# Seven-product stage one of a mixture of experts: product 4 ahead of product 3, product 2 summed onto product 4's PSUM bank

## The chip, the cores and the metric

The kernel runs on one core of a Trainium2 chip. The metric is the device time of one execution in microseconds (us). Before the change the median of three runs is 2261.65 us (2260.79 to 2263.05).

The engines are TensorE (PE; its weight loads are shown apart as PEld), VectorE (DVE), ScalarE (ACT), GpSimd (POOL) and SyncE (SP), which only issues transfers here. PSUM is the memory that the matmuls write; the kernel uses it as eight banks of 128 x 512 fp32.

## The reference

Attention with a block mask on 4 x 8 heads of 768 tokens gives x, 3072 tokens of 512 features. A mixture of 8 experts follows, with every token sent to every expert, and with gate weights P that are balanced by rows and columns in eight rounds:

```python
for e in range(E):
    h = np.maximum(x @ w1[e], 0.0)
    ye = h @ w2[e]
    out += P[:, e:e + 1] * ye
```

w1[e] is 512 x 1024, w2[e] is 1024 x 512.

## The kernel before

The attention fills the first 422 us of the profile. The rest, to 2257 us, is the mixture of experts, of which the change touches the first product, x @ w1.

**The arithmetic.** Both products are taken as 2 x 2 blocks by a scheme of seven products in place of eight (numbered 0 to 6), with sums and differences of blocks ahead and behind. Every operand is kept as an fp16 high half and an fp16 low half, and a product is the sum of three passes, high by high, high by low and low by high.

**Items, quarters, products.** The work is cut into 32 items i, which are expert e = i // 4 and batch b = i % 4. `stage1(i, qi)` makes a quarter of an item, 128 of the 512 columns of a block. Its seven products, in the order 0, 1, 5, 6, 3, 4, 2, are six matmuls of 128 x 384 each (L1200) into a bank of the pool `ps_h`, which has four banks and in which a tile is a product (`p4_0_1` is product 4 of quarter 1 of item 0). `comb` (L1212) is VectorE's `scalar_tensor_tensor`: PSUM times 2^-20 plus a tile in SBUF. With P0 to P6 the products:

- a1 = P0 (ScalarE, L1247); r11 = P1 + a1; a1 = a1 + P5; u3 = P6 + a1
- c21 = P3 + u3; then two combs read product 4's bank: u3 = P4 + u3 and a1 = P4 + a1
- a1 = P2 + a1
- relu of r11, u3, a1 (L1251, L1267, L1271); `add` makes the four sums that stage two needs on GpSimd (L1274, L1086).

These tiles come from a pool of eight (`fresh`). `emit(n, src)` turns one of them into an operand of stage two, a tile h out of 30: the high half on ScalarE (L1222), the low half on VectorE (L1226, L1232) or, for 2, 3 and 5, on GpSimd.

`stage2(i, p)` (L1302) takes product p of the second stage in three tiles `py`, twelve matmuls of 128 x 256 each (L1317), into the pool `ps_y`, the other four banks; VectorE adds them to the output (L1340, tiles `acc`).

**The order of the work.** The main loop runs stage two of item i, its products 0, 1, 5, 6, 3, 4, 2, with the four quarters of item i + 1 between them. Lazy work is placed by `Slots`, a planner in Python: `tick(n, m)` charges a product 0.976 us of TensorE, 0.55 n of VectorE and 0.5 m of ScalarE, and queued work is handed out when the engines' charges leave room. That work is: the low halves; the balance of the gate (L1144 to 1180); and, once an expert, the *exchange* of weights. In an exchange w1 or w2 of the next expert is loaded (L177, 2 MB), its largest magnitude is taken in eight pieces on ScalarE (L108, tile `mx_w`), reduced on VectorE (L194, `ma_w`), spread over the partitions by TensorE (L114, `all_w`), and made a scale (L200 to 206). Then each of the seven sums of weight blocks is split into halves, the high one on ScalarE (L1064) and the low one on VectorE (L1068), as `w1p` (in `arena` and `attic`) and `w2p`. At an exchange of w1 the split of product p is queued by `used[p]()`, behind the matmuls of product p that use the old weights. While these sit in the queues, the inputs of the last batch are split too (L355 on ScalarE, L356 on VectorE, tiles `xs_3`), at the start of stage one. Each item's x is loaded by SyncE in the order 0, 1, 5, 6, 3, 4, 2 (L227).

Behind the planner a scheduler reorders the instructions of each engine by its own costs; the order shown below is what comes out of both. An engine runs its instructions in that order, one after the other, each when the semaphores of its operands allow.

## Time and profile before

| | |
|---|---|
| median of three runs | 2261.65 us |
| span of the profiled execution, its own time from first to last instruction | 2260.3 us |
| stage one of the experts begins | 422 us |
| TensorE busy | 2168.3 us (96%) |
| VectorE busy | 1873.6 us (83%) |
| ScalarE, GpSimd busy | 1314.1 us, 1326.1 us |
| mean granted TensorE clock | 0.995 |

The profile is of one execution. A row of a group gives line, engine, operation, out<-in, its shape and count, then busy time, the mean time of one in nanoseconds, and the idle time of the engine ahead of them with what ended it. Rows of the timeline give start, duration and operation, and in brackets the idle time ahead and its releaser. Names are the program's without numbers: `p<-attic` is a product of stage one, `a<-p,a` a comb. Matmuls overlap, so the duration of a single one is longer than the spacing of a row of them. "PEclk" and the clock of a window are the share of TensorE's full clock that was granted.

### The profile page before, as it was taken

To read this page: it belongs to the slowest core of one execution; us is meant where nothing else is said; L and a number is where in the kernel's file an instruction comes from. 1 tells how busy PE (TensorE), PEld (TensorE's weight loads), DVE (VectorE), ACT (ScalarE), POOL (GpSimd) and SP (SyncE) were. 2 spreads that over 40 slices of the span, in tenths; PEclk is the share of its full clock that TensorE was granted. 3 is DMA by queue.
4 is the path that set the end of the run, shared out by engine and by line. 5 is a ranking of instruction groups with operands and counts; after the bars stand their busy time and mean duration, and the time that the engine had idled before them with its cause. 6 is when DMAs were issued, how large, how long until landed. Compare 5 with 4: busy or idle time off the path is not lost.

```text
span 2260.3 us, 47619 instructions
## 1 busy us (share of the span) xinstructions
PE 2168.3 (96%) x18892; PEld 1599.6 (71%) x18892; DVE 1873.6 (83%) x3289; ACT 1314.1 (58%) x2431; POOL 1326.1 (59%) x1369
## 2 busy tenths in 40 slices
PE   6999999899988999999999999999999999999999
PEld 4777667567775777677777777777777777777777
DVE  7889999787888878887888788878887888788876
ACT  6888889664457544654465446544654465446442
POOL 3124456585549564866486548655866586658553
PEclk9999999999999999999999999999999999999999
DMA  7766965313122212121212121212121212121221
GB/s 165 143 151 144 203 134 134 115 57 115 50 63 74 87 50 69 68 88 50 86 51 87 50 87 50 87 50 87 50 87 50 87 50 87 50 87 57 78 78 50
DMA packets 195347, 192.36 MB, mean 85 GB/s; under 512 B 132124, under 2 KB 150580, under 8 KB 195124
## 3 DMA queue, kind: packets, MB, share of 16 engines
q1 hardware_dynamic: 194560, 189.30, 29.0%
q8 instruction: 147, 2.41, 0.4%
q14 instruction: 76, 0.62, 0.1%
q10 hardware_dynamic: 564, 0.03, 0.0%
HBM read 140.54 MB, written 17.30 MB: 70 GB/s over the span
## 4 chain that ended last, share of the span: by engine, by line
PE 71%; DVE 11%; POOL 10%; ACT 4%; issue 3%; DMA 1%; SPq 0%; POOLq 0%; DVEq 0%; ACTq 0%
PE p L1200 30%; PE py L1317 30%; POOL r L1079 3%; PE u L760 3%; DVE acc L1340 2%; PE t L705 2%; PE m L669 2%; PE m L672 2%; PE t L702 2%; POOL h L1232 2%; DVE top L678 1%; DVE attic L1068 1%; DVE h L1232 1%; POOL s L1274 1%; POOL a L1086 1%
## 5 line engine op out<-in xcount | busy, mean ns | idle before, releaser
L1317 PE MATMUL py<-w2p,h 128*128 128x256 f16 x8064 | 945.0, 273 | 31.2 <-DVE acc L1340 14.7
L1317 PEld LDWEIGHTS <-h 128*128 128x128 f16 x8064 | 787.7, 98 | 165.7 <-issue 32.2
L1340 DVE SCALAR_TENSOR_TENSOR acc<-py,spare,acc 128x256 f32<-128x256 f32 (+1 forms) x840 | 456.1, 580 | 64.5 <-PE py L1317 60.0
L1232 POOL TENSOR_TENSOR h<-u,h 128x384 f16<-128x384 f32 x128 | 119.8, 936 | 578.4 <-ACT h L1222 578.3
L1200 PEld LDWEIGHTS <-attic 128*128 128x128 f16 x3072 | 300.6, 98 | 198.2 <-issue 19.9
L1200 PE MATMUL p<-attic 128*128 128x384 f16 x2304 | 411.5, 326 | 11.2 <-DVE a L1212 5.3
L1200 PE MATMUL p<-arena 128*128 128x384 f16 x2304 | 413.3, 328 | 5.1 <-DVE arena L1068 4.2
L1200 PEld LDWEIGHTS <-arena 128*128 128x128 f16 x2304 | 226.4, 99 | 140.9 <-issue 7.4
L1222 ACT ACTIVATE h<-c 128x384 f16<-128x384 f32 x256 | 133.0, 520 | 316.2 <-DVE c L1212 240.7
L1212 DVE SCALAR_TENSOR_TENSOR a<-p,a 128x384 f32<-128x384 f32 x384 | 210.8, 549 | 21.3 <-PE p L1200 17.1
L678 DVE TENSOR_REDUCE top<-m 128x1 f32<-128x768 f32 x192 | 181.7, 950 | 31.4 <-PE m L672 30.9
L710 ACT ACTIVATE pe<-t,qk 128x768 int32<-128x768 f32 x192 | 172.1, 899 | 45.3 <-PE t L705 42.3
L1222 ACT ACTIVATE h<-r 128x384 f16<-128x384 f32 x256 | 132.3, 519 | 66.4 <-POOL r L1086 61.9
L1086 POOL TENSOR_TENSOR c<-c,r 128x384 f32<-128x384 f32 x128 | 159.9, 1249 | 10.0
L1086 POOL TENSOR_TENSOR r<-s,r 128x384 f32<-128x384 f32 x128 | 153.8, 1201 | 10.0
L1212 DVE SCALAR_TENSOR_TENSOR r<-p,a 128x384 f32<-128x384 f32 x128 | 70.7, 552 | 95.1 <-PE p L1200 71.2
L1200 PE MATMUL p<-arena,attic 128*128 128x384 f16 x768 | 146.0, 326 | 3.3 <-DVE a L1212 3.3
L1274 POOL TENSOR_TENSOR s<-a,u 128x384 f32<-128x384 f32 x128 | 134.4, 1050 | 21.8 <-ACT a L1271 21.8
L1222 ACT ACTIVATE h<-s 128x384 f16<-128x384 f32 x128 | 66.7, 521 | 134.6 <-POOL s L1274 134.5
L1086 POOL TENSOR_TENSOR a<-a,r 128x384 f32<-128x384 f32 x128 | 135.5, 1059 | 9.5
L1079 POOL TENSOR_TENSOR r<-r 128x256 f32<-128x256 f32 (+1 forms) x106 | 119.7, 1148 | 34.4 <-DVE arena L1068 33.2
L1232 POOL TENSOR_TENSOR h<-r,h 128x384 f16<-128x384 f32 x128 | 136.9, 1070 | 3.8 <-ACT h L1222 2.8
(205 smaller groups left out, 3723.5 us busy)
## 6 DMA issues: line engine op xcount, KB each, us to landing
arena<-xd SPq DMA_DIRECT2D x128, 384.0 KB, 4.0
attic<-xd SPq DMA_DIRECT2D x96, 384.0 KB, 4.3
r<-in_moe_w_dram SPq DMA_DIRECT2D x16, 2048.0 KB, 8.9
arena<-in_q_dram SPq DMA_DIRECT2D x16, 384.0 KB, 4.2
arena<-in_k_dram SPq DMA_DIRECT2D x16, 384.0 KB, 4.4
arena<-in_v_dram SPq DMA_DIRECT2D x4, 1536.0 KB, 8.2
xd<-xs_t SPq DMA_DIRECT2D x16, 384.0 KB, 3.5
out_dram<-acc SPq DMA_DIRECT2D x48, 128.0 KB, 1.7
```

The costliest lines, as they stand in the source:

```text
L678: nc.vector.tensor_reduce(out=tops[n][:, c : c + 1], in_=sc[:, :S], axis=AX.X, op=ALU.max)
L710: nc.scalar.activation(pe, sc[:, :S], AF.Exp, bias=EXP_SHIFT, scale=qk[n // 2][3])
L760: nc.tensor.matmul(uv[:, c], lhsT=l[:, c * P : (c + 1) * P], rhs=w[:, h, kc, :], start=(kc == 0 and c == 0 and m == 0), stop=(kc == NC - 1 ...
L1079: lambda c=c: Pinned.gpsimd.tensor_tensor(out=out[:, c], in0=x[:, c], in1=y[:, c], op=op),
L1086: nc.gpsimd.tensor_tensor(out=out, in0=x, in1=y, op=ALU.subtract)
L1200: nc.tensor.matmul(ps, lhsT=w1p[p][:, l, kc, fs], rhs=xp[p][:, r, kc], start=(kc == 0 and m == 0), stop=(kc == KH - 1 and m == 2),)
L1212: nc.vector.scalar_tensor_tensor(out=t, in0=ps, scalar=HDOWN, in1=other, op0=ALU.mult, op1=ALU.add)
L1222: nc.scalar.activation(h[:, 0], src, AF.Relu if relu else AF.Copy)
L1232: eng.tensor_tensor(out=h[:, 1], in0=src, in1=h[:, 0], op=ALU.subtract)
L1274: nc.gpsimd.tensor_tensor(out=s1, in0=a1, in1=u3, op=ALU.add)
L1317: nc.tensor.matmul(py, lhsT=hs[i, p, kc][:, l, tsl], rhs=w2p[p][:, r, kc], start=(kc == 0 and m == 0), stop=(kc == KF // 2 - 1 and m == 2),)
L1340: nc.vector.scalar_tensor_tensor(out=dst, in0=src, scalar=c, in1=dst, op0=ALU.mult, op1=ALU.add)
```

## The change

Product 4 is taken ahead of product 3. It is combined into a new tile c22 = P4 + u3, whose relu and high half follow at once; c21 = P3 + u3 is then written over u3. Product 2 opens no bank of its own: its matmuls add to what stands in product 4's bank (`start=False`), once the comb of c22 has read it, and one comb a1 = (P4 + P2) + a1 takes the place of two. A quarter has one comb less, 128 in all, and takes six banks and not seven; the number of matmuls and of tiles stays. The planner is charged for it: `tick(2, 2)` and `tick(1, 1)` become `tick(1, 2)` and `tick(1, 1)`, 0.55 less of VectorE a quarter.

```diff
@@ -1192,14 +1192,17 @@
         fs = slice(qi * P, (qi + 1) * P)
         lop = LOPE if i < NLE else LOP
 
-        def product(p):
+        def product(p, ps=None):
             slots.need(("w1", i // B, p))
-            ps = ps_h.tile([P, 512], F32, tag="ph", name=f"p{p}_{i}_{qi}")[:, :TH]
+            opens = ps is None
+            if opens:
+                ps = ps_h.tile([P, 512], F32, tag="ph", name=f"p{p}_{i}_{qi}")[:, :TH]
             for kc in range(KH):
                 for m, (l, r) in enumerate(((0, 0), (0, 1), (1, 0))):
                     nc.tensor.matmul(
                         ps, lhsT=w1p[p][:, l, kc, fs], rhs=xp[p][:, r, kc],
-                        start=(kc == 0 and m == 0), stop=(kc == KH - 1 and m == 2),
+                        start=(opens and kc == 0 and m == 0),
+                        stop=(kc == KH - 1 and m == 2), skip_group_check=True,
                     )
             if used and p in used:
                 used[p]()
@@ -1257,21 +1260,21 @@
         comb(u3, product(6), a1)
         tick(1, 0)
         slots.settle(i, qi - 1)
-        c21 = fresh("c21")
+        c22 = fresh("c22")
+        p4 = product(4)
+        comb(c22, p4, u3)
+        nc.scalar.activation(c22, c22, AF.Relu)
+        emit(3, c22)
+        tick(1, 2)
+        c21 = u3
         comb(c21, product(3), u3)
         emit(1, c21, relu=True)
         tick(1, 1)
-        p5 = product(4)
-        comb(u3, p5, u3)
-        comb(a1, p5, a1)
-        nc.scalar.activation(u3, u3, AF.Relu)
-        emit(3, u3)
-        tick(2, 2)
-        comb(a1, product(2), a1)
+        comb(a1, product(2, p4), a1)
         nc.scalar.activation(a1, a1, AF.Relu)
 
         def add():
-            nc.gpsimd.tensor_tensor(out=s1, in0=a1, in1=u3, op=ALU.add)
+            nc.gpsimd.tensor_tensor(out=s1, in0=a1, in1=c22, op=ALU.add)
             sub(a1, a1, r11)
             slots.need((("h", i, 0), i, qi))
             sub(r11, s1, r11)
```

By the edit the planner hands work out at other places, and the scheduler orders all engines anew. Three places are shown, of before and then of after. In the changed kernel lines below L1195 have numbers higher by two or three (L1212 becomes L1215, L1340 becomes L1343); product 2's matmuls and comb carry the tile of product 4.

First, ScalarE at the first exchange of w2 (expert 0 to 1, `mx_w2_1`), at the end of item 4's stage one. `h` are high halves, `acc` the scaling of the output. Before, from the high half of quarter 4_3's c21 on:

```order
L1222 ACTIVATE h_15_8087<-c21_4_3_11290 128x384
L1267 ACTIVATE u3_4_3_11279<-u3_4_3_11279 128x384
L1222 ACTIVATE h_0_8072<-c21_4_2_11118 128x384
L108 ACTIVATE unread_80,mx_w2_1_10773<-r2_1_10770 128x512
L1271 ACTIVATE a1_4_3_11251<-a1_4_3_11251 128x384
L1222 ACTIVATE h_23_8095<-u3_4_3_11279 128x384
L1279 ACTIVATE c21_4_3_11290<-c21_4_3_11290 128x384
L1323 ACTIVATE acc_0_8102<-acc_0_8102,spare_3_10729 128x512 x2
L108 ACTIVATE unread_80,mx_w2_1_10773<-r2_1_10770 128x512
```

After, from the high half of quarter 4_1's a1 on, past the last L108:

```order
L1225 ACTIVATE h_16_8088<-a1_4_1_10859 128x384
L1225 ACTIVATE h_14_8086<-r11_4_2_11053 128x384
L1225 ACTIVATE h_18_8090<-r11_4_1_10869 128x384
L108 ACTIVATE unread_80,mx_w2_1_10741<-r2_1_10738 128x512
L1225 ACTIVATE h_0_8072<-u3_4_1_10896 128x384
L1266 ACTIVATE c22_4_2_11083<-c22_4_2_11083 128x384
L108 ACTIVATE unread_80,mx_w2_1_10741<-r2_1_10738 128x512
L1225 ACTIVATE h_27_8099<-u3_4_2_11072 128x384
L1225 ACTIVATE h_8_8080<-c22_4_2_11083 128x384
L1282 ACTIVATE u3_4_2_11072<-u3_4_2_11072 128x384
L1274 ACTIVATE a1_4_2_11044<-a1_4_2_11044 128x384
L1250 ACTIVATE a1_4_3_11215<-p0_4_3_11216 128x384
```

The last L108 of `mx_w2_1` stood behind the relu of quarter 4_3's c21 and a scaling of acc; it stands behind c22 of 4_2, ahead of a1 of 4_3.

Second, VectorE at the start of stage one, around the end of quarter 1 of item 0. Before:

```order
L1212 SCALAR_TENSOR_TENSOR u3_0_1_8216<-p4_0_1_8239,u3_0_1_8216 128x384
L1212 SCALAR_TENSOR_TENSOR a1_0_1_8181<-p4_0_1_8239,a1_0_1_8181 128x384
L204 RECIPROCAL sw2_0_7715<-ma_w2_0_7714 128x1
L1226 SCALAR_TENSOR_TENSOR h_8_8080<-c21_0_1_8227,h_8_8080 128x384
L1212 SCALAR_TENSOR_TENSOR a1_0_1_8181<-p2_0_1_8251,a1_0_1_8181 128x384
L205 TENSOR_SCALAR sw2_0_7715<-sw2_0_7715 128x1
L206 TENSOR_SCALAR iw2_0_7716<-ma_w2_0_7714 128x1
L1353 TENSOR_SCALAR pc_0_10725<-iw1_0_4252,iw2_0_7716 128x1
L1355 TENSOR_SCALAR pcb_0_10727<-inv_v_72,pc_0_10725 128x4
L356 TENSOR_TENSOR xs_3_b10_9225<-xf_3_6802,xs_3_b10_9225 128x768
L356 TENSOR_TENSOR xs_3_b01_9276<-xf_3_6802,xs_3_b01_9276 128x768
L1212 SCALAR_TENSOR_TENSOR r11_0_2_8276<-p1_0_2_8277,a1_0_2_8266 128x384
```

After:

```order
L1215 SCALAR_TENSOR_TENSOR c22_0_1_8225<-p4_0_1_8226,u3_0_1_8214 128x384
L1358 TENSOR_SCALAR pcb_0_10519<-inv_v_72,pc_0_10517 128x4
L1235 TENSOR_TENSOR h_4_8076<-a1_0_0_8104,h_4_8076 128x384
L1215 SCALAR_TENSOR_TENSOR u3_0_1_8214<-p3_0_1_8237,u3_0_1_8214 128x384
L356 TENSOR_TENSOR xs_3_b10_9026<-xf_3_6802,xs_3_b10_9026 128x768
L356 TENSOR_TENSOR xs_3_b01_9077<-xf_3_6802,xs_3_b01_9077 128x768
L1215 SCALAR_TENSOR_TENSOR a1_0_1_8179<-p4_0_1_8226,a1_0_1_8179 128x384
L1229 SCALAR_TENSOR_TENSOR h_9_8081<-u3_0_1_8214,h_9_8081 128x384
L356 TENSOR_TENSOR xs_3_b11_9080<-xf_3_6802,xs_3_b11_9080 128x768
L1215 SCALAR_TENSOR_TENSOR r11_0_2_8272<-p1_0_2_8273,a1_0_2_8262 128x384
L1215 SCALAR_TENSOR_TENSOR a1_0_2_8262<-p5_0_2_8286,a1_0_2_8262 128x384
```

The two L356 stood behind the comb of product 2 and ahead of product 1's of the next quarter; they stand ahead of product 2's comb (`a1_0_1<-p4_0_1`), and a third L356 stands behind it.

Third, VectorE at a later exchange (w2 of expert 4). Before, from the reduction (L194) to the first steps of the scale:

```order
L194 TENSOR_REDUCE ma_w2_4_18868<-mx_w2_4_18867 128x1
L1212 SCALAR_TENSOR_TENSOR r11_16_3_19357<-p1_16_3_19358,a1_16_3_19348 128x384
L1212 SCALAR_TENSOR_TENSOR a1_16_3_19348<-p5_16_3_19369,a1_16_3_19348 128x384
L1232 TENSOR_TENSOR h_21_8093<-r11_16_3_19357,h_21_8093 128x384
L1212 SCALAR_TENSOR_TENSOR u3_16_3_19377<-p6_16_3_19378,a1_16_3_19348 128x384
L1212 SCALAR_TENSOR_TENSOR c21_16_3_19386<-p3_16_3_19387,u3_16_3_19377 128x384
L1212 SCALAR_TENSOR_TENSOR u3_16_3_19377<-p4_16_3_19399,u3_16_3_19377 128x384
L1212 SCALAR_TENSOR_TENSOR a1_16_3_19348<-p4_16_3_19399,a1_16_3_19348 128x384
L1226 SCALAR_TENSOR_TENSOR h_19_8091<-c21_16_3_19386,h_19_8091 128x384
L1212 SCALAR_TENSOR_TENSOR a1_16_3_19348<-p2_16_3_19411,a1_16_3_19348 128x384
L200 TENSOR_REDUCE ma_w2_4_18868<-all_w2_4_19397 128x1
L201 TENSOR_SCALAR ma_w2_4_18868<-ma_w2_4_18868 128x1
```

After:

```order
L194 TENSOR_REDUCE ma_w2_4_18739<-mx_w2_4_18738 128x1
L1215 SCALAR_TENSOR_TENSOR u3_16_2_19073<-p3_16_2_19095,u3_16_2_19073 128x384
L1343 SCALAR_TENSOR_TENSOR acc_3_9915<-py_15_4_0_19119,spare_6_16614,acc_3_9915 128x256 x2
L1229 SCALAR_TENSOR_TENSOR h_8_8080<-u3_16_2_19073,h_8_8080 128x384
L1343 SCALAR_TENSOR_TENSOR acc_3_9915<-py_15_4_1_19135,spare_6_16614,acc_3_9915 128x256 x2
L1215 SCALAR_TENSOR_TENSOR a1_16_2_19043<-p4_16_2_19083,a1_16_2_19043 128x384
L1343 SCALAR_TENSOR_TENSOR acc_3_9915<-py_15_4_2_19152,spare_6_16614,acc_3_9915 128x256 x2
L1343 SCALAR_TENSOR_TENSOR acc_3_9915<-py_15_2_0_19172,spare_6_16614,acc_3_9915 128x256
L1235 TENSOR_TENSOR h_25_8097<-s1_16_2_19113,h_25_8097 128x384
L1235 TENSOR_TENSOR h_16_8088<-a1_16_2_19043,h_16_8088 128x384
L1343 SCALAR_TENSOR_TENSOR acc_3_9915<-py_15_2_1_19188,spare_6_16614,acc_3_9915 128x256
L200 TENSOR_REDUCE ma_w2_4_18739<-all_w2_4_19170 128x1
```

The reduction stood ahead of quarter 16_3's combs, and the scale behind them; the reduction stands in quarter 16_2, and the scale ahead of 16_3's combs.

## The prediction

> **What bounds the kernel now.** The page comes first: how long, and which engine is never free.
>
> ```profile
> span 2260.3 us, 47619 instructions
> PE 2168.3 (96%) x18892; PEld 1599.6 (71%) x18892; DVE 1873.6 (83%) x3289; ACT 1314.1 (58%) x2431; POOL 1326.1 (59%) x1369
> L1212 DVE SCALAR_TENSOR_TENSOR a<-p,a 128x384 f32<-128x384 f32 x384 | 210.8, 549 | 21.3 <-PE p L1200 17.1
> ```
>
> TensorE is busy 96% of the span. The change takes no matmul away, so it can gain only where TensorE waits, or where its clock falls. The VectorE operation that it takes away is one of the third row's kind: 0.549 us, 128 times, 70.3 us in all, nearly all of it beside matmuls. The second view is TensorE's waits over the mixture of experts, 420 to 2260 us (columns: total, times, longest).
>
> ```profile
> PE py L1317 <- DVE acc L1340: 14.7, 11, 1.7
> PE p L1200 <- DVE a L1212: 9.5, 8, 2.7
> PE py L1317 <- DVE w2p L1068: 8.1, 7, 1.7
> PE all_w L114 <- DVE ma_w L194: 7.3, 1, 7.3
> PE py L1317 <- ACT w2p L1064: 6.6, 8, 1.0
> PE p L1200 <- DVE arena L1068: 4.2, 6, 1.9
> PE p L1200 <- ACT a L1247: 2.8, 3, 1.3
> PE p L1200 <- DVE r L1212: 2.3, 6, 1.1
> ```
>
> These sum to 55.5 us in 50 waits: that, and what the clock loses, is the ceiling of any gain. The third view is busy time by stretch (columns: stretch, length, PE, PEld, DVE, ACT, POOL, granted clock, DMA share, GB/s).
>
> ```profile
> 442.00:452.00 10.00, 5.37 (x27) 2.88 (x27) 9.31 (x14) 6.68 (x14) 9.84 (x8) 0.86 0.11 41
> 452.00:462.00 10.00, 10.00 (x51) 5.45 (x50) 8.46 (x16) 6.66 (x15) 8.22 (x9) 0.80 0.69 221
> 700.00:706.00 6.00, 0.00 (x0) 0.00 (x0) 3.65 (x6) 5.54 (x15) 5.02 (x6) 0.65 0.37 125
> 706.00:712.00 6.00, 5.60 (x18) 2.80 (x19) 5.42 (x13) 6.00 (x12) 5.84 (x8) 0.50 0.00 0
> 980.00:1100.00 120.00, 120.00 (x927) 90.46 (x925) 90.74 (x170) 57.37 (x121) 69.44 (x66) 1.00 0.20 68
> 1202.00:2100.00 898.00, 879.34 (x6707) 655.10 (x6705) 744.38 (x1304) 468.93 (x950) 578.16 (x544) 1.00 0.20 69
> ```
>
> Between exchanges of weights (980 to 1100) TensorE is busy all the time, and nothing is to be had there. What is lost lies at the start of stage one, at the first exchange of experts, and in a few microseconds at each later exchange. So the change is costed at those places, and VectorE's 70.3 us by themselves at nothing: matmuls cover them, and they cost only where VectorE is late for TensorE.
>
> **The change, part by part.**
>
> *A, the start (433 to 470 us).* TensorE's waits there, and, in the timeline (start, length, operation), VectorE's work ahead of the two longest:
>
> ```profile
> PE p L1200 <- DVE a L1212: 3.2, 3, 2.2
> PE p L1200 <- ACT a L1247: 1.6, 2, 1.3
> PE p L1200 <- DVE r L1212: 1.1, 1, 1.1
> ```
>
> ```profile
> 443.68 2.81 DVE L356 TENSOR_TENSOR xs_b<-xf,xs_b 128x768 f16<-128x768 f32 x2 [0.62 <-ACT xs_b L355]
> 446.41 0.54 DVE L1212 SCALAR_TENSOR_TENSOR r<-p,a 128x384 f32<-128x384 f32 x1
> ...
> 447.68 2.16 DVE L1232 TENSOR_TENSOR h<-a,h 128x384 f16<-128x384 f32 x1
> 449.76 0.54 DVE L1212 SCALAR_TENSOR_TENSOR a<-p,a 128x384 f32<-128x384 f32 x1
> ```
>
> 5.9 us of waiting: two L356 of the input's last batch (2.81 us) stand ahead of the comb that empties product 1's bank, and then a low half of 2.16 us ahead of the next. In the new order (second piece of the order above) the two stand between product 3's comb and product 2's. By TensorE's new order products 0, 1 and 2 of about 1 us each run meanwhile, so they cover 2.9 us. The comb of product 1 still comes late: after product 3's matmuls end, VectorE does one comb (0.56 with some 0.14 before it), 2.81, a comb of 0.54, a low half of about 1, a third L356 of about 1.4 (half of 2.81) and the comb (0.54), 7.0 us. The matmuls that need its bank, product 3 of that quarter, stand six products behind, 5.8 us. That leaves 1.2 us, so I take 4.7 us off. If the low half is again 2.16 us the gain is 3.5; if all waits go, 5.9.
>
> The clock: in the rows 442 to 462 it stood at 0.86 and 0.80, which loses 1.4 + 2.0 = 3.4 us less what falls into idle time, some 3.0. With one wait of a microsecond left I take half off, 1.5 (bounds 0 and 3.0). [...]
>
> *B, the first exchange (698.8 to 712 us).* TensorE stands 7.3 us (the fourth of the waits above) for the scale of the second expert's w2:
>
> ```profile
> 705.45 0.61 ACT L108 ACTIVATE unread<-r 128x512 bf16<-128x512 f32 x1
> 706.19 0.16 DVE L194 TENSOR_REDUCE ma_w<-mx_w 128x1 f32<-128x8 f32 x1 [2.53 <-ACT unread L108]
> ```
>
> The last of ScalarE's eight L108 ends it. The planner charges VectorE 0.55 less a quarter, so lazy work is handed out sooner; the first piece of the order above shows that the last L108 now stands behind c22 of quarter 4_2, and not behind c21 of 4_3: almost a quarter earlier, seven products of 0.98 us (three take 1307.08 to 1310.01 in part D), 6.8 us. Besides, TensorE now has product work mixed with the last matmuls of stage two of item 3, where before it ran quarters 4_0 to 4_3 bare. The 7.3 us go (bound: 0, if the load of w2, which starts behind the last split of w1, comes no earlier and ends last). With them goes the clock at 0.50 in the row 706 to 712, 5.60 busy, half lost: 2.8 us. [...] B is 10.1 us.
>
> *C, the six later exchanges.* One stretch that holds five of them, 1098 to 2100, and around one of them a split of w2 on VectorE and two of TensorE's waits:
>
> ```profile
> PE py L1317 <- DVE acc L1340: 8.5, 5, 1.7
> PE py L1317 <- DVE w2p L1068: 6.0, 5, 1.2
> PE py L1317 <- ACT w2p L1064: 4.9, 5, 1.0
> PE p L1200 <- DVE arena L1068: 2.2, 5, 0.5
> PE p L1200 <- DVE r L1212: 1.2, 5, 0.2
> ```
>
> ```profile
> 1400.53 1.83 DVE L1068 SCALAR_TENSOR_TENSOR w2p<-r,sw,w2p 128x1024 f16<-128x1024 f32 x1
> ```
>
> ```profile
> 1402.42 3.76 PE L1317 MATMUL py<-w2p,h 128*128 128x256 f16 x33 [1.20 <-DVE w2p L1068]
> 1416.36 1.47 PE L1317 MATMUL py<-w2p,h 128*128 128x256 f16 x12 [1.69 <-DVE acc L1340]
> ```
>
> 22.8 us in five, 4.56 each. The third piece of the order above shows the scale of w2 (L194, L200) now in quarter 16_2, ahead of 16_3's combs, and not around those, so the splits have more matmuls ahead of their first use, more than the 1.20 and 1.0 waited. I let both kinds of w2p wait go, 2.2 an exchange. The acc wait comes from VectorE being busy just then; I let half of its 1.7 go, 0.85. The other two (0.7) stay. Against that an order that is new places other operands just in time: the old one left 4.56 an exchange, I charge a quarter of that, 1.1. Net 1.95 an exchange, six times, 11.7 us (bounds: 27.4 if all waits go, and a loss of 6.6 if none goes and the 1.1 is paid).
>
> *D, one bank fewer.* Product 2 adds to product 4's bank, so it must wait for c22's comb, and the bank stays taken until product 2's comb. How long that takes with VectorE idle is seen in quarters without other work:
>
> ```profile
> 1307.08 3.09 PE L1200 MATMUL p<-arena 128*128 128x384 f16 x18
> 1310.01 1.14 PE L1200 MATMUL p<-arena,attic 128*128 128x384 f16 x6
> ```
>
> ```profile
> 1310.21 0.56 DVE L1212 SCALAR_TENSOR_TENSOR a<-p,a 128x384 f32<-128x384 f32 x1 [0.34 <-PE p L1200]
> ```
>
> Three products end at 1310.17 and the next one starts 0.16 us before that; the last one's comb ends at 1310.77. A product that needed the bank of the one just before it would so lose about 0.8 us, with VectorE idle. Between products 4 and 2 stand product 3 (0.98) and mostly 17 matmuls of stage two (3.76/33 = 0.11 each, 1402.42 above), 2.8 us, so the first wait costs nothing. The second is near: in five places of the bare quarters (0_0 to 0_3, and 4_2) product 6 of the next quarter takes the bank that product 2 has left one product before, 0.98 us of cover for 0.8. A low half ahead of the comb (0.5 to 2.16) makes a wait of it: I take 0.6 each, 3.0 us (bounds 0, and 5 x 2.0 = 10). In the later items the nearest such pair has 2.6 us between, more than before the change, since a quarter takes six banks and not seven. The same six also loosen waits for banks elsewhere; I count nothing for that.
>
> *At nothing:* product 4 ahead of product 3 moves the queueing of its w1 split and nothing in the order of SyncE's loads of x; both run ahead of need. If a load landed just in time for product 3, product 4 would lose up to 0.98 us an item; against it, no wait of a product for a transfer stands among the waits above. The relu of c22, the sum's other operand and the low halves keep their kinds and numbers; matmuls cover them. `start=False` changes no size. At the end of the program the last item has stage two alone behind it.
>
> *The sum:* -4.7 - 1.5 - 10.1 - 11.7 + 3.0 = -25.0. The profiled execution spans 2260.3, the median of the three runs is 2261.65, which is 1.35 more and lies around the span, so 2261.65 - 25.0 = 2236.7.
>
> **The rivals.** *No change:* every later exchange re-makes its waits in other places (C worth 0), and the waits that lie outside A, B and C (55.5 - 5.9 - 7.3 - 27.4 = 14.9 us), which I left as they are, nearly double by the new order, 12 more. Then A and B, -16.3, + 3.0 + 12 = -1.3, 2260. For it: the order is planned by costs that left 50 waits before. Against: VectorE has 128 operations less. *Slower:* product 2's comb comes late on VectorE, and the next quarter's product waits for the bank not five times but in most quarters. The loss decides over the 25.0 gained when a quarter waits 0.2 us on the mean (25.0/128); at 0.35 it costs 44.8, less 3.0 counted, 2278. For it: low halves of w2p take 1.83 and those of h 2.16, more than half of the cover of 2.6. Against: in 1098 to 2100 no wait for a bank's comb of product 2 shows, and VectorE was busy 744.38 of 898 us and will be less. *A larger gain:* A's clock returns fully, and the exchanges lose nearly all of their 27.4 us: -25.0 - 1.5 - 14 = -40.5, and 2221.
>
> **How the numbers follow.** A measurement of this kernel tells 0.2%, 4.5 us, from no change, so "same" is 2257.1 to 2266.2. The forecast (2237, all within 2224 to 2252): 0.63. No change: 0.13, of which 0.02 falls on the faster side. Slower: 0.09. Larger gain: 0.15. Faster is thus 0.63 + 0.15 + 0.02 = 0.80, same 0.11, slower 0.09. The range reaches down to 2221, which leaves out half of the larger gain (0.075), and up to 2259, which leaves out the slower case and the upper part of no change (about 0.13).
>
> **What would show it.** Right: no wait of all_w for ma_w near 700 and a clock of 1.00 there; the waits of py for w2p gone or under 0.5 us; VectorE's busy time 70 us lower, 1803; TensorE's busy time still 2150 to 2170, at 97%. Wrong: new waits of p for the comb of a behind product 2, a wait for a w2p split that moved too, or ScalarE standing for the load of w2 with L108 at its head.

## The result and the profile after

The changed kernel takes 2275.3 us (median of four runs, 2274.91 to 2275.68), the kernel before 2262.35 beside it on the same chip (2260.79 to 2264.12). The ratio is 1.0056, 95% interval 1.0042 to 1.0071: 13 us slower, where 25 us faster was forecast. The profiled execution spans 2273.8 us, 13.5 more than before.

The page's first lines after:

```profile
span 2273.8 us, 47337 instructions
PE 2174.2 (96%) x18892; PEld 1601.5 (70%) x18892; DVE 1871.2 (82%) x3161; ACT 1320.0 (58%) x2431; POOL 1326.0 (58%) x1369
```

VectorE has 128 operations less, and is busy for 2.4 us less, not 70. TensorE's waits over the mixture of experts, after:

```profile
PE p L1202 <- DVE r L1215: 16.7, 13, 2.0
PE p L1202 <- DVE c L1215: 14.1, 13, 1.8
PE p L1202 <- DVE a L1215: 10.4, 10, 2.9
PE py L1320 <- DVE acc L1343: 8.3, 8, 1.8
PE p L1202 <- DVE u L1215: 4.1, 6, 1.4
PE p L1202 <- ACT a L1250: 2.4, 2, 1.7
PE py L1320 <- DVE w2p L1068: 1.7, 3, 0.8
...
PE py L1320 <- ACT w2p L1064: 1.0, 1, 1.0
```

The wait of all_w, 7.3 us, is gone, and the waits of py for w2p and acc have shrunk from 29.4 to 11.0 us. In their place stage one's products (p) wait for combs: r, c, a and u together 45.3 us, where r, a and u were 12.5 before. The stretch with five of the later exchanges shows it purest. Of the five rows of before, 22.8 us in all, only the wait for r is left, and it has grown from 1.2 us:

```profile
PE p L1202 <- DVE r L1215: 13.1, 10, 2.0
PE p L1202 <- DVE c L1215: 9.8, 9, 1.5
PE p L1202 <- DVE a L1215: 4.2, 5, 0.9
PE p L1202 <- DVE u L1215: 2.7, 5, 0.5
PE py L1320 <- POOL h L1235: 1.5, 5, 0.5
```

Together 31.3 us. Timelines of one exchange show where they come from. VectorE and TensorE (start, length, operation):

```profile
1420.64 1.41 DVE L1343 SCALAR_TENSOR_TENSOR acc<-py,spare,acc 128x512 f32<-128x512 f32 x2
1421.96 1.88 DVE L1068 SCALAR_TENSOR_TENSOR w2p<-t,sw,w2p 128x1024 f16<-128x1024 f32 x1
1423.76 1.34 DVE L1235 TENSOR_TENSOR h<-s,h 128x384 f16<-128x384 f32 x1
1425.03 1.34 DVE L1235 TENSOR_TENSOR h<-a,h 128x384 f16<-128x384 f32 x1
1426.30 0.55 DVE L1215 SCALAR_TENSOR_TENSOR r<-p,a 128x384 f32<-128x384 f32 x1
```

```profile
1423.75 1.14 PE L1202 MATMUL p<-attic 128*128 128x384 f16 x6
1426.89 1.14 PE L1202 MATMUL p<-attic 128*128 128x384 f16 x6 [2.01 <-DVE r L1215]
```

The low half of w2 (1.88 us) and two low halves of h (1.34 each) stand ahead of the comb r, which is to empty product 1's bank. Product 3 needs that bank and TensorE stands 2.0 us. Some 50 us earlier product 2 waits for c22's comb, which must have read product 4 before product 2 may add to its bank:

```profile
1368.58 0.56 DVE L1215 SCALAR_TENSOR_TENSOR r<-p,a 128x384 f32<-128x384 f32 x1 [2.47 <-ACT a L1250]
1369.06 1.34 DVE L1235 TENSOR_TENSOR h<-s,h 128x384 f16<-128x384 f32 x1
1370.32 1.35 DVE L1235 TENSOR_TENSOR h<-a,h 128x384 f16<-128x384 f32 x1
...
1373.43 0.56 DVE L1215 SCALAR_TENSOR_TENSOR c<-p,u 128x384 f32<-128x384 f32 x1
```

```profile
1374.04 1.14 PE L1202 MATMUL p<-attic 128*128 128x384 f16 x6 [1.54 <-DVE c L1215]
```

Product 3 and 17 matmuls of stage two did stand between, as forecast; VectorE was later than those 2.8 us. But no low half of the weights stands ahead of this comb. VectorE had stood idle for 2.47 us, waiting for ScalarE's copy of product 0 (the bracket in the first row), and then did two low halves of h. ScalarE was late because it had stood 2.53 us for the load of w2 with the first L108 at the head of its queue; from there on it worked without a gap, through all eight L108, up to the copy:

```profile
1358.82 0.63 ACT L108 ACTIVATE unread<-r 128x512 bf16<-128x512 f32 x1 [2.53 <-DMA r<-in_moe_w_dram]
...
1367.39 0.63 ACT L108 ACTIVATE unread<-r 128x512 bf16<-128x512 f32 x1
...
1368.02 0.47 ACT L1250 ACTIVATE a<-p 128x384 f32<-128x384 f32 x1
```

The load is issued at 1349.04, when the last low half of w1 has freed its buffer (1348.97), and lands at 1358.80. ScalarE's waits for this load from 775 us on, after and then before:

```profile
ACT unread L108 <- DMA r<-in_moe_w_dram: 9.9, 6, 2.5
```

```profile
ACT unread L108 <- DMA r<-in_moe_w_dram: 0.2, 1, 0.2
```

This is one of the signs that the prediction named for being wrong. Last the clock, in windows (columns as in the prediction): the two places that the prediction spoke of, and two of the later exchanges.

```profile
442.00:452.00 10.00, 6.95 (x32) 3.62 (x32) 9.76 (x12) 4.87 (x11) 8.80 (x9) 0.83 0.23 82
452.00:462.00 10.00, 9.71 (x60) 5.67 (x58) 8.14 (x13) 7.68 (x18) 9.77 (x9) 1.00 0.81 248
700.00:706.00 6.00, 6.00 (x46) 4.27 (x44) 5.87 (x9) 6.00 (x12) 5.84 (x6) 1.00 0.01 3
706.00:712.00 6.00, 6.00 (x44) 4.14 (x43) 6.00 (x9) 3.15 (x8) 6.00 (x9) 1.00 0.01 3
1184.00:1204.00 20.00, 17.94 (x125) 12.70 (x123) 19.66 (x30) 10.21 (x19) 11.57 (x11) 0.91 0.08 19
1414.00:1434.00 20.00, 17.95 (x138) 13.26 (x136) 19.66 (x30) 10.25 (x19) 11.75 (x11) 1.00 0.07 14
```

At 700 to 712 TensorE is busy at full clock, where it stood before. Around the new wait of 2 us the clock is down at some of the later exchanges: 0.91 over 20 us, which loses up to 1.8 us.

To compare kernels by stretch, the table below sums for each the time by which a matmul starts later behind the one before than is usual (162 ns behind one of stage one, 109 ns behind one of stage two). The some 130 other matmuls count with the usual spacing of their kind; how these are grouped shifts the first column by up to 1 us and the others by some 0.4 us. The sums hold waits and lost clock together; the number of matmuls is the same in all.

| us lost in | 425 to 525 | 525 to 775 (first exchange) | 775 to 1000 | from 1000 on | sum |
|---|---|---|---|---|---|
| before | 16.6 | 21.4 | 8.5 | 31.6 | 78.1 |
| after | 14.7 | 14.1 | 13.5 | 49.1 | 91.3 |

The start and the first exchange gave 9 us, and the six later exchanges (one before 1000, five behind) took 22.

### The profile page after: what moved, and what is told of

Read it like the earlier page. It is cut to its first block, busy times and chain, and to the rows that moved or that the text cites. A ratio compares the mean times of both kernels' runs of the same rounds, so it can differ in the third digit from the quotient of the medians.

```text
span 2273.8 us, 47337 instructions
## 1 busy us (share of the span) xinstructions
PE 2174.2 (96%) x18892; PEld 1601.5 (70%) x18892; DVE 1871.2 (82%) x3161; ACT 1320.0 (58%) x2431; POOL 1326.0 (58%) x1369
## 3 DMA queue, kind: packets, MB, share of 16 engines
q1 hardware_dynamic: 194560, 189.30, 29.4%
## 4 chain that ended last, share of the span: by engine, by line
PE 66%; DVE 13%; ACT 7%; POOL 6%; issue 4%; DMA 4%; SPq 0%; DVEq 0%; POOLq 0%; ACTq 0%
PE py L1320 29%; PE p L1202 26%; DMA r<-in_moe_w_dram 3%; PE u L760 3%; DVE acc L1343 2%; DVE h L1235 2%; PE t L705 2%; ACT unread L108 2%; PE m L669 2%; PE m L672 2%; PE t L702 2%; ACT h L1225 2%; DVE top L678 1%; POOL r L1079 1%; DVE u L1215 1%
## 5 line engine op out<-in xcount | busy, mean ns | idle before, releaser
L1320 PE MATMUL py<-w2p,h 128*128 128x256 f16 x8064 | 956.6, 274 | 13.3 <-DVE acc L1343 8.3
L1343 DVE SCALAR_TENSOR_TENSOR acc<-py,spare,acc 128x256 f32<-128x256 f32 (+1 forms) x840 | 457.6, 583 | 54.0 <-PE py L1320 52.2
L1202 PE MATMUL p<-attic 128*128 128x384 f16 x2304 | 425.5, 327 | 33.4 <-DVE r L1215 16.7
L1235 POOL TENSOR_TENSOR h<-c,h 128x384 f16<-128x384 f32 x128 | 122.5, 957 | 372.7 <-ACT h L1225 372.6
L1202 PEld LDWEIGHTS <-arena 128*128 128x128 f16 x2304 | 224.9, 98 | 150.1 <-issue 14.6
L1277 POOL TENSOR_TENSOR s<-a,c 128x384 f32<-128x384 f32 x128 | 128.9, 1007 | 243.7 <-ACT a L1274 243.7
L678 DVE TENSOR_REDUCE top<-m 128x1 f32<-128x768 f32 x192 | 182.0, 952 | 32.1 <-PE m L672 31.6
L1266 ACT ACTIVATE c<-c 128x384 f32<-128x384 f32 x128 | 66.9, 523 | 243.1 <-DVE c L1215 242.9
L1225 ACT ACTIVATE h<-u 128x384 f16<-128x384 f32 x256 | 132.3, 518 | 88.8 <-POOL u L1086 58.4
L1215 DVE SCALAR_TENSOR_TENSOR a<-p,a 128x384 f32<-128x384 f32 x256 | 141.3, 552 | 44.8 <-PE p L1202 40.1
L1225 ACT ACTIVATE h<-r 128x384 f16<-128x384 f32 x256 | 130.2, 520 | 56.6 <-POOL r L1086 53.5
L1086 POOL TENSOR_TENSOR u<-u,r 128x384 f32<-128x384 f32 x128 | 156.4, 1222 | 10.0
L1235 DVE TENSOR_TENSOR h<-a,h 128x384 f16<-128x384 f32 x128 | 135.1, 1055 | 9.5 <-ACT h L1225 8.4
L1079 POOL TENSOR_TENSOR r<-r 128x256 f32<-128x256 f32 (+1 forms) x106 | 130.7, 1251 | 17.5 <-DVE arena L1068 17.5
```

What stands on the lines that cost most here:

```text
L678: nc.vector.tensor_reduce(out=tops[n][:, c : c + 1], in_=sc[:, :S], axis=AX.X, op=ALU.max)
L1079: lambda c=c: Pinned.gpsimd.tensor_tensor(out=out[:, c], in0=x[:, c], in1=y[:, c], op=op),
L1086: nc.gpsimd.tensor_tensor(out=out, in0=x, in1=y, op=ALU.subtract)
L1202: nc.tensor.matmul(ps, lhsT=w1p[p][:, l, kc, fs], rhs=xp[p][:, r, kc], start=(opens and kc == 0 and m == 0), stop=(kc == KH - 1 and m == 2 ...
L1215: nc.vector.scalar_tensor_tensor(out=t, in0=ps, scalar=HDOWN, in1=other, op0=ALU.mult, op1=ALU.add)
L1225: nc.scalar.activation(h[:, 0], src, AF.Relu if relu else AF.Copy)
```

## The experiments

The theory at first: product 2 keeps product 4's bank taken, so that fewer banks circulate and every late comb stops TensorE (the bank theory). Its rivals: the planner's lower charge hands out the splits of weights too early, ahead of combs (planner, later queue theory); product 4 ahead of product 3 is what costs (order theory); and, formed on the way, that the 13 us are chance of one planned order.

| kernel | median us | ratio to before beside it, 95% interval | us lost from 1000 on |
|---|---|---|---|
| tick_back | 2273.8 | 1.0051, 1.0036 to 1.0066 | 45.7 |
| swap_only | 2268.4 | 1.0029, 1.0017 to 1.0040 | 39.7 |
| share_only | 2259.4 | 0.9990, 0.9981 to 0.9999 | 31.0 |
| share_two | 2286.6 | 1.0106, 1.0089 to 1.0123 | 50.2 |
| charge_only | 2263.7 | 1.0007, 0.9998 to 1.0016 | 40.0 |
| after_nolow | 2208.2 | 0.9759, 0.9744 to 0.9773 | 4.0 |
| before_nolow | 2221.4 | 0.9818, 0.9804 to 0.9833 | 5.6 |
| after_53 | 2250.9 | 0.9944, 0.9928 to 0.9961 | 28.6 |
| before_53 | 2281.4 | 1.0082, 1.0067 to 1.0098 | 53.5 |
| share_53 | 2268.9 | 1.0023, 1.0012 to 1.0034 | 38.2 |
| before_jit (0.99) | 2259.3 | 0.9985, 0.9975 to 0.9994 | 32.2 |
| after_jit (0.99) | 2266.0 | 1.0015, 1.0006 to 1.0024 | 35.7 |
| before_j96 (0.96) | 2267.7 | 1.0024, 1.0014 to 1.0033 | 32.3 |
| after_j96 (0.96) | 2251.1 | 0.9949, 0.9934 to 0.9963 | 32.7 |
| before_j101 (1.01) | 2256.1 | 0.9972, 0.9961 to 0.9982 | 32.4 |
| after_j101 (1.01) | 2261.6 | 0.9997, 0.9987 to 1.0006 | 37.7 |
| after53_j99 | 2258.9 | 0.9988, 0.9978 to 0.9997 | 33.2 |
| after53_j96 | 2262.6 | 1.0002, 0.9992 to 1.0012 | 36.5 |

### One part of the change at a time

**tick_back**, the changed kernel with the old charge:

```diff
         emit(3, c22)
-        tick(1, 2)
+        tick(2, 2)
```

> The changed kernel, with the planner's charge for product 4 put back to two combs (tick(2, 2)); order of products and shared bank stay. Bank theory (product 2 keeps product 4's bank taken, so fewer banks circulate and a late VectorE comb stops TensorE): the waits of p for the combs c, r, a, u stay near the changed kernel's 45 us, time 2268 to 2278. Planner theory (the charge of 0.55 less hands weight splits out too early, ahead of combs): most of the 13 us comes back, 2258 to 2265, and waits of py for w2p return. Order theory (product 4 ahead of product 3 is itself what costs): 2268 to 2278.

2273.8 us, as bank and order theory had it. But the waits are others:

```profile
PE py L1320 <- DVE acc L1343: 23.3, 12, 2.9
PE p L1202 <- DVE a L1215: 14.3, 18, 1.9
PE py L1320 <- DVE w2p L1068: 9.6, 8, 1.5
PE p L1202 <- DVE c L1215: 3.3, 8, 0.9
PE all_w L114 <- DVE ma_w L194: 3.3, 1, 3.3
```

Those for combs are 19.3 us and not 45, those for w2p are back, and acc has the most. ScalarE's wait for the load of w2 is down to 0.2 us from 775 us on. The total is what two theories gave, but the waits are not those that the bank theory names.

**swap_only**, the order alone:

```diff
+        comb(a1, p4, a1)
         emit(3, c22)
-        tick(1, 2)
+        tick(2, 2)
...
-        comb(a1, product(2, p4), a1)
+        comb(a1, product(2), a1)
```

> Product 4 ahead of product 3 alone: product 2 opens its own bank again, two combs read product 4, charged as two. Bank theory: the waits of p for c fall from 14 us to under 3 and the time is 2255 to 2264, at or under the kernel before. Planner theory: likewise near the kernel before, 2258 to 2266. Order theory: 2268 to 2278.

2268.4 us, 6 over before: at the lower end of the order theory's range, and above those of the other two. No wait for c is among its rows; acc takes 25.1 us, and all_w again 7.1.

**share_only**, product 3 first and product 2 on product 4's bank:

```diff
-        c22 = fresh("c22")
+        c21 = fresh("c21")
+        comb(c21, product(3), u3)
+        emit(1, c21, relu=True)
+        tick(1, 1)
+        c22 = u3
         p4 = product(4)
         comb(c22, p4, u3)
...
         tick(1, 2)
-        c21 = u3
-        comb(c21, product(3), u3)
-        emit(1, c21, relu=True)
-        tick(1, 1)
         comb(a1, product(2, p4), a1)
```

> Product 3 ahead of product 4 as before, product 2 on product 4's bank, one comb, charged as one. Product 2 stands right behind product 4, so wherever no matmul of stage two is put between them TensorE waits some 0.8 us for the comb. Bank theory: the worst of these four, over 2275, with waits of p for u (the comb that reads product 4) of 10 us or more. Planner theory: as the changed kernel, 2268 to 2278, since the charge is the same. Order theory: near the kernel before, 2258 to 2266.

2259.4 us, 3 under before. The bank theory made it the worst of the four and it was the best; the wait for u came as foreseen (12.2 us), but no more in sum. In this form the bank theory falls; the order theory's range holds it.

**share_two**, share_only with `tick(2, 2)` in place of `tick(1, 2)`:

> As share_only, but with the planner charged two combs for product 4. Tells the charge from the sharing: with the old order of products the charge alone made the first exchange some 7 us shorter and the later ones some 8 us longer. If the charge does the same here, the first exchange's wait of all_w is back at 7 us and the later exchanges lose 20 to 25 us in place of 31: 2252 to 2260. If the later exchanges' losses only shift by chance of the order, they may lie either way, 2252 to 2270.

2286.6 us, 27 over share_only, far outside of what was expected, though only one number in the planner differs. The first exchange's wait of all_w was 0.9 us and not 7, where share_only with the lower charge has 3.2, and acc took 20.7.

**charge_only**, the kernel before with `tick(1, 2)`:

> The kernel before with nothing changed but the planner's charge for product 4, one comb in place of two (tick(1, 2)). Planner theory: 2268 to 2278, with waits of p for combs at the exchanges as in the changed kernel. Bank theory and order theory: 2255 to 2264, since work handed out earlier brings the waits for w2p and the first exchange's 7.3 us down and no bank is held.

2263.7 us, no change. By stretch it is a gain and a loss: the first exchange loses 14.0 in place of 21.4 (all_w waits 1.5), the later ones 40.0 in place of 31.6. With the old products the charge is thus what moved the scale of w2 forward, as the prediction said; share_only and share_two show no such rule. A wait for r of 10.3 us stands here as well. At this constant the largest new wait of the changed kernel is thus seen in two of the three kernels with the lower charge, and in none of the four with the old one (2.3 us at most). The charge alone does not make the 13 us, since the first exchange gains what the later ones lose.

The order theory's ranges hold tick_back, swap_only, share_only and charge_only. It falls with share_two, which has the old order and is the slowest kernel here, and with after_j96 below, which has the new order and is 16.6 us under its partner.

### What the late combs wait behind

**after_nolow** and **before_nolow** leave out the low halves of the weights of experts 1 to 7, in the changed kernel and in the one before; the planner is charged as ever, and four fifths of VectorE's other operations keep their place in its order. VectorE has 98 operations less in each:

```diff
-        slots.add(
-            lambda: Pinned.vector.scalar_tensor_tensor(
-                out=dst[:, 1], in0=src, scalar=s, in1=dst[:, 0],
-                op0=ALU.mult, op1=ALU.subtract,
-            ),
-            key, 1, True, dve=1.55,
-        )
+        def low():
+            if key[1] == 0:
+                Pinned.vector.scalar_tensor_tensor(
+                    out=dst[:, 1], in0=src, scalar=s, in1=dst[:, 0],
+                    op0=ALU.mult, op1=ALU.subtract,
+                )
+
+        slots.add(low, key, 1, True, dve=1.55)
```

> The changed kernel, in which the low halves of the weights (L1068) of experts 1 to 7 are not computed; the planner is charged for them as ever. That takes 90 operations of 1.5 us off VectorE, all at the exchanges. Queue theory (the change moved these splits ahead of the combs): the waits of p for combs at the later exchanges fall from 6 us an exchange to under 2, and the time is within 4 us of the same removal made in the kernel before. Bank theory: it stays 8 us or more behind that kernel.

> The kernel before without the low halves of the weights of experts 1 to 7: the control of the last. Both theories: the waits of py for w2p by VectorE (8.1 us) go and those for acc (14.7) shrink, 2238 to 2254.

2208.2 and 2221.4 us. Of all waits from 775 us on, one row is left in the changed kernel, and one in the kernel before:

```profile
PE p L1203 <- DVE r L1216: 0.4, 1, 0.4
```

```profile
PE p L1201 <- ACT a L1248: 2.5, 6, 0.4
```

This is the clearest of the runs. Without the low halves of the weights on VectorE nearly every wait at the later exchanges is gone, before and after. By the traces they act in two ways: directly, where one stands in the queue ahead of a comb (the 2.0 us wait for r), and by way of the load of w2, which waits for the last low half of w1; without them ScalarE stands for that load 0.5 us from 775 us on, and not 9.9. No run separates the two ways, and the removal also takes 139 us of work off VectorE (1871.2 to 1732.2), which may shorten other queues.

Without them the changed kernel is 13 us ahead (2221.4 - 2208.2): 10.3 of that in 525 to 775 (4.7 lost against 15.0), where all_w's 7.2 us are gone, and the rest at the start and behind. So in this order of work the gain that was forecast for B is there, and what turns the sign lies at the later exchanges. Two expectations failed: both kernels were to come within 4 us of each other, and the one before was to take 2238 to 2254.

### Five banks

**after_53** and **before_53** give stage one five banks and stage two three:

```diff
-    ps_h = mpool("ps_h", 4, space=PSUM)
-    ps_y = mpool("ps_y", 4, space=PSUM)
+    ps_h = mpool("ps_h", 5, space=PSUM)
+    ps_y = mpool("ps_y", 3, space=PSUM)
```

> The changed kernel with five banks for stage one's products and three for stage two's tiles, in place of four and four. Bank theory (product 2 holds product 4's bank across product 3, so with four banks a comb that is late stops TensorE): the waits of p for combs (45 us) fall by half or more, the time is under 2268 unless stage two's waits for acc grow by as much. Order theory (the reordering puts low halves ahead of combs on VectorE whatever the banks): the waits of p for combs stay within a quarter of 45 us, 2270 or more.

> The kernel before with five and three banks: the control. Both theories: the waits of py for acc grow from 14.7 us, as stage two has a bank less; 2262 to 2275. If it gets faster, stage one was short of banks before the change too.

2250.9 and 2281.4 us. In the changed kernel the waits for r, a and u fell as the bank theory said; the wait for c, for product 4's own bank, stayed:

```profile
PE p L1202 <- DVE c L1215: 11.2, 12, 1.7
PE py L1320 <- DVE acc L1343: 11.1, 10, 3.7
PE p L1202 <- DVE r L1215: 4.5, 6, 0.7
PE p L1202 <- DVE a L1215: 4.3, 2, 3.3
```

In the kernel before, stage two pays for its bank, 36.4 us of waits for acc, and the time lies over the 2262 to 2275 that were expected. That looked like proof. Two more values of the planner's constant (below) say less.

**share_53**, share_only with five and three:

> Product 3 ahead of product 4 as before, product 2 on product 4's bank, one comb, charged as one, with five banks for stage one and three for stage two. With four banks this order measured 0.1% under the kernel before, and its waits of p were for the combs u (12.2 us: product 2 right behind product 4, and it must wait for product 4's comb) and a (13.0). Bank theory: the fifth bank takes waits for a down by half, but not those for u, which are for product 4's own bank: 2248 to 2258. If the reorder has no worth of its own, it is at or under the changed kernel with five banks, 2250.9; if product 3 between 4 and 2 is the cover that it should be, it is over that by 3 us or more.

2268.9 us: 9 over share_only, and outside its range. The wait for u stayed (14.6), the one for a fell (2.1); w2p took 13.5.

### How much is chance of the order

One constant of the planner is shifted, the cost of a product on TensorE, and nothing else:

```diff
-            slots.tick(0.976, 0.55 * n, 0.5 * m)
+            slots.tick(0.99, 0.55 * n, 0.5 * m)
```

> The kernel before, with the planner's cost of a product on TensorE at 0.99 in place of 0.976 and nothing else: how much a change of order without meaning moves the time. If the later exchanges' losses are set by where single operands happen to fall, 3 to 10 us either way of 2262; if by the structure, within 3 us.

> The changed kernel with the same shift of the planner's cost. If the 13 us are chance of one order, this falls as well under 2262 as over it; if they come of late combs and a held bank, it stays 6 us or more over the kernel before, 2268 to 2284, with waits of p for c and r again the largest.

> The kernel before with the planner's cost of a product at 0.96. By chance of placement alone it lies within 8 us of 2262 either way.

> The changed kernel with the same value. If the change costs by itself: 3 to 15 us over before_j96, with 8 us or more of waits of p for c (product 2 waiting for c22's comb). If the 13 us were chance: as likely under before_j96 as over it.

> The kernel before with the planner's cost of a product at 1.01: within 8 us of 2262 either way.

> The changed kernel with the same value. If the change costs by itself: 3 to 15 us over before_j101, with 8 us or more of waits of p for c. If the 13 us were chance: as likely under it as over it.

| constant | before | after | difference |
|---|---|---|---|
| 0.976 (the kernels as they are) | 2262.35 | 2275.3 | +13.0 |
| 0.99 | 2259.3 | 2266.0 | +6.7 |
| 0.96 | 2267.7 | 2251.1 | -16.6 |
| 1.01 | 2256.1 | 2261.6 | +5.5 |

The four differences have a mean of 2.1 us, and scatter by 12.9 (standard deviation), which leaves the mean uncertain by 6.5. At 0.96 the changed kernel was expected 3 to 15 us over its partner, if the change costs by itself, and is 16.6 under it; at 1.01 it came as that expectation has it, 5.5 over, with 8.7 us of waits for c. At 0.99 it was expected 6 us or more over, at 2268 or more, and is 6.7 over at 2266, with the waits for c and a the largest and the one for r all but gone. The waits of the changed kernel at 0.96:

```profile
PE py L1320 <- ACT w2p L1064: 16.6, 13, 1.8
PE py L1320 <- DVE w2p L1068: 9.6, 8, 1.5
PE p L1202 <- DVE c L1215: 5.4, 4, 1.9
PE py L1320 <- DVE acc L1343: 4.7, 11, 1.6
PE p L1202 <- DVE a L1215: 3.9, 4, 1.9
```

No row for r is left, which was the largest at 0.976 (16.7 us; 0.9 at 0.99 and at 1.01). In all four of the changed kernel the wait for c is there (14.1, 12.6, 5.4, 8.7 us). The start and the first exchange together lose less than in their partner in three of four (28.8 against 38.0, 22.2 and 41.3, 28.5 and 31.7); at 0.99 they are about equal (32.8 and 34.1, within what the way of counting shifts).

At the later exchanges the four pairs tell more than the totals do. From 775 us on:

| constant | us lost, before | us lost, after | ScalarE's wait for the load of w2, after | TensorE's wait for c, after |
|---|---|---|---|---|
| 0.976 | 40.1 | 62.6 | 9.9 | 11.4 |
| 0.99 | 41.3 | 48.4 | 9.9 | 9.7 |
| 0.96 | 40.8 | 42.2 | none | 1.2 |
| 1.01 | 40.8 | 50.3 | 10.9 | 7.8 |

The kernel before hardly moves there; what moves it is the start and the first exchange. The changed kernel loses more in every pair, by 22.5, 7.1, 1.4 and 9.5 us, 10.1 on the mean, uncertain by 4.5. And product 2's wait for c22 is large where ScalarE stands for the load and small where it does not. The other kernels that have both the new order and the shared bank agree: 0.2 and 1.6 us in tick_back, 6.5 and 9.1 in after_53, 6.7 and 9.0 in after53_j99, 0.4 and none in after53_j96. That an earlier load, or later L108, would take this wait away was not tried.

**after53_j99** and **after53_j96**, the changed kernel with five and three banks at two of these values:

> The changed kernel with five and three banks and the planner's cost of a product at 0.99, to be set beside after_jit (four and four, 2266). If the fifth bank is what helps: under 2260, with waits of p for r, a and u together under 12 us. If 2250.9 was chance: as likely over 2262 as under.

> The same at 0.96, to be set beside after_j96. If the fifth bank helps: 5 us or more under after_j96. If 2250.9 was chance: as likely over it as under.

2258.9 and 2262.6 us: 7 under its partner with four banks, as a helping bank would have it, and 11.5 over. With the 24 us under it at 0.976, the fifth bank moves the time by -24.4, -7.1 and +11.5, -6.7 on the mean. That the banks help is not shown, and 2250.9 is not a version to trust more than after_j96 with four banks, 2251.1, which is as fast: both beat the two kernels of this case, but each stands for one order of work.

## Why the prediction was wrong

**A, the start:** -6.2 was forecast, waits and clock. From 425 to 525 the loss fell by 1.9, known to about 1 us. The clock came back in part, as reckoned (0.86 and 0.80 became 0.83 and 1.00: 1.7 of the 3.4 us). The waits of products there fell from 5.9 to 3.9, not to 1.2, and stage two's of w2p, 1.6 us, now fall into that stretch (before, 1.2 us of them stood just behind it).

**B, the first exchange:** -10.1 was forecast, and at its place it came: the reduction stands at 695.5 and not 706.19, all_w waits no more, the clock is 1.00. Over 525 to 775 the loss fell by 7.3, as new waits for acc, c and u stand around it.

**C, the later exchanges:** this is the step that failed. It said that both w2p waits and half of the acc wait go, and charged 1.1 us an exchange for what a new order brings: -11.7. Of the old waits nearly all went, some 22 us in five exchanges, more than it said. But new ones came, 31.3 us, 6.3 an exchange where 1.1 was charged: the waits moved from stage two's operands to stage one's banks. Of the 6.3 the wait for r of 2.0 us has a low half of the weights just ahead of its comb. The waits for c, 9.8 us in five exchanges, begin at ScalarE, which now stands for the load of w2; low halves of h and combs queue up behind that on VectorE. Ahead of the smaller waits (r 0.6, a 0.85, u 0.54) stand the steps of the scale, acc and low halves of h. With the clock of the exchanges behind 1000 (5.2 us by windows of 25 us, none before) and the exchange near 950 this makes +22 in place of -11.7, where the worst bound given was +6.6. In all four orders the loss there rose, where it was to fall.

**D, one bank fewer:** product 2's wait for c22 was put at nothing, under a cover of 2.8 us with VectorE idle, and the next quarter's wait at 3.0. The first is 14.1 us in 13 waits. The cover is as long as was said; what failed is that VectorE is idle and its inputs are there. Between exchanges it has time, and there the change indeed costs nothing (TensorE is busy for 120.00 of the 120 us from 980 on, as before). At the exchange shown above 5.7 us of queue (1420.64 to 1426.30) stand ahead of the comb r, and a wait of 2.47 us for ScalarE with 2.7 us of low halves ahead of c22's.

**The rivals:** the slower one named the right resource, combs that come late behind low halves, and the wrong frequency: not in most quarters, but a few times at each exchange, and not product 2's comb alone. That its 2278 lies near the 2275.3 measured is luck. The larger part of the error lies under all of them: neither the forecast nor a rival put its new waits at the later exchanges, and a shift of a constant without meaning moves this kernel by 24 us (2251.1 to 2275.3), the one before by 12. The sign of this change could not be had from parts that are worth less than that.

**What is settled and what not.** Shown: the waits at the later exchanges go when the weights' low halves on VectorE go (both nolow kernels); product 2 waits for c22 in each of four orders, most where ScalarE stands for the load of w2; the scale of w2 comes in time at the first exchange in the changed kernel, and nearly so in charge_only. Likely, with the same sign in four orders: the changed kernel loses more at the later exchanges, by 10.1 us on the mean, uncertain by 4.5. Not shown: that the change as a whole costs or gains; its mean over four orders is +2.1 us, uncertain by 6.5. Some 10 of the 13 us belong to this one order, above all the wait for r, which the other three of the changed kernel all but lack. That a bank held longer is what costs stays open: five banks took 24 us off in one order, 7 in another, and added 11.5 in the third.

## What to carry to other kernels

Where a planner and a scheduler place work anew, measure an edit at several values of a constant that should not matter, before and after, and compare means, stretch by stretch; one pair told +13 us here and another -17, while the later exchanges had one sign in all four. Where an operation is taken off an engine that waits nowhere for itself, look not at its total but at the stretch where its queue is long, and list what then stands ahead of the operations that free a buffer: work handed out earlier is also work in front of something. Follow a late operation back past its own engine: here the chain ran from TensorE to VectorE, to ScalarE, and to a load that had not landed. A cover of matmuls holds only if the engine that it covers comes to the operation in time.

## What was not expected of the hardware

**VectorE's time did not fall with its work.** The combs taken out are 70 us, and VectorE is busy for 2.4 us less. Three groups of low halves after (before: 921, 862 and 727 ns a piece):

```profile
L1235 DVE TENSOR_TENSOR h<-a,h 128x384 f16<-128x384 f32 x128 | 135.1, 1055 | 9.5 <-ACT h L1225 8.4
L1235 DVE TENSOR_TENSOR h<-s,h 128x384 f16<-128x384 f32 x128 | 120.1, 939 | 21.8 <-ACT h L1225 20.2
L1235 DVE TENSOR_TENSOR h<-r,h 128x384 f16<-128x384 f32 x128 | 98.4, 769 | 20.7 <-ACT h L1225 20.6
```

All 512 low halves of h took 443.9 us and not 401.4, which is the largest part of what came back. They read two tiles in SBUF, and single ones of these three groups took from 0.54 to 1.39 us; combs, which read one of their operands from PSUM, took 0.55 in both kernels. GpSimd is busy 1326.0 us (58%) after and 1326.1 (59%) before. In the trace after, the 55 of these 384 low halves that had no GpSimd operation beside them took 0.54 to 0.56 us each; the 263 that had one beside them for nine tenths of their length or more took 0.55 to 1.39, 1.06 on the mean (before: 234, 0.97 on the mean). The combs kept to 0.56 or less with GpSimd at work and without. No run tried whether the one slows the other.

**The clock fell at some of equal waits.** The five exchanges after 1100 have the same wait of 2 us at the same place and 17.9 of 20 us busy; the clock was 0.91 at three (1184, 1869, 2098) and 1.00 at two (1414, 1642). The traces show what differs. Where the clock fell it was 0.50 for 3.41 us, and the starts of these stretches (968.29, which belongs to the exchange before 1000, 1196.98, 1883.06, 2111.76) lie 228.69, 686.08 and 228.70 us apart: 67, 201 and 67 times the 3.413 us that one lasts. At these the wait lies whole within the 3.41 us ahead, of which TensorE was busy for 1.39 to 1.41:

```profile
1193.56:1196.98 3.42, 1.41 (x8) 0.77 (x8) 3.31 (x5) 2.45 (x4) 3.34 (x4) 1.00 0.00 0
1196.98:1200.39 3.41, 3.41 (x16) 2.11 (x14) 3.31 (x5) 1.83 (x4) 0.85 (x1) 0.50 0.00 0
```

Counted on in the same steps, a step ends at 1425.67 and at 1654.36, within the waits at the two other exchanges (1424.88 to 1426.89, 1652.70 to 1654.71). Of the two steps that meet there, TensorE is busy for 2.58 and 2.19 us at 1425.67 and for 1.70 and 3.06 at 1654.36, and the clock stays at 1.00. At the six later exchanges of this trace the fall thus came four times behind a step that held a wait of 2.0 us whole, and at neither of the two waits that an end of a step divides; no run moved a wait against the steps to try it.
